# Later q/k load, shorter float64 conversion and earlier weight fetches in a fused attention and low-rank-mixing MLP kernel

## The chip, the cores and the metric

The kernel runs on one core of a Trainium2 chip. The time is device microseconds of one execution; 817.39 us is the median of three executions (816.22 to 820.38).

## What is computed

Attention with a relative-position bias runs over 4 batches, 8 heads, 576 positions and 64 channels a head; its result, with heads side by side, goes through a low-rank mixing over positions and a two-layer MLP, each with a residual.

```python
scores = scale * q @ k.T                                # per batch and head
x = log1p(|i - j|) / log1p(max(i, 1))
scores += (maximum(x * w1 + b1, 0.0) @ w2)[head]        # 32 hidden units
attn = exp(scores - max); attn = attn / (attn.sum() + 1e-09)
x = concat_heads(attn @ v)                              # [4, 576, 512] float32
u = x + (x.T @ U @ V).T                                 # U, V are float64, rank 32
out = float32(u + maximum(u @ w_ch1, 0.0) @ w_ch2)      # weights are float64
```

The float64 arrays (U, V and both weights, 512 by 2048 and 2048 by 512) come to the chip as pairs of 32-bit words and are turned into float32 there.

## The kernel before, in words

The kernel has an order written out by hand. Each engine works through its own instructions in that order, and SyncE (SP) issues all DMAs in one queue, so that a DMA that waits holds up those behind it.

The bias stage comes first. 36 steps (the loop over `order`) each make four `ring` tiles of hidden units (one on ScalarE, three on VectorE, `bias_hid`), multiply them with `w2` on TensorE (`bias_mm`), scale on ScalarE and store to `bias_dram` (`bias_out`). `bias_loads` fetches the bias again, in the order that attention wants, when the rows are there. Slots 0 to 3 of head pair 0 are woven into this loop (`early`).

Attention then works through 16 pairs of heads (four a batch), nine slots each. `load_pair` brings q and k of a pair into the tile `raw`, of which there is one buffer. `prep_ops` splits it into a rounded part (`hi`) and a remainder (`lo`) in four steps, on GpSimd for all pairs but pair 0, into tiles with two buffers. `scores` multiplies, adds the bias and takes the extreme on VectorE; `exps` takes the exponential and its sum on ScalarE; `recip` adds 1e-9 to the sums and inverts them (slots 0, 4 and 8) and scales the 64 left-over rows of the pair into `pm` on GpSimd. Transposes (`tr`, `tr_m`, `tr_mid`), the product with v (`av`) and `assemble` follow in later slots. After every slot `background(1)` emits one group from `queue`.

`queue` holds the float64 conversions, 256 columns each. `conv_ops` makes one: a load into `wraw` (three buffers), `size`, `clamp`, `shift`, `join` and `power` on VectorE, `low` on ScalarE, `scale` and `add` on GpSimd. `pipeline` makes five groups of each. 20 of them run beside attention (U, V and the first quarter of the weights, which goes to `wq_dram`), 48 beside the MLP stage, with two groups a step.

Pairs 5, 9, 13 also carry the mixing of the batch before (`mix_t`, `mix_h`, whose result goes to `u_dram`). From pair 13 on `first_weights` fetches the converted first quarter again from `wq_dram`, and `split` makes its two parts on ScalarE and GpSimd. The MLP stage (`mlp1`, `mlp2`) goes over nine blocks of 256 rows for each of four quarters.

Of the kernel before, what the change touches and what calls it, by code (L numbers as in the profile page):

```python
# [8 lines left out]
F32 = mybir.dt.float32  # L9
F32R = mybir.dt.float32r  # L10
I32 = mybir.dt.int32
# [31 lines left out]
def kernel(  # L43
# [34 lines left out]
    const = ctx.enter_context(tc.tile_pool(name="const", bufs=1, side="left"))  # L78
    qkp = ctx.enter_context(tc.tile_pool(name="qkp", bufs=2, side="left"))
    wcp = ctx.enter_context(tc.tile_pool(name="wcp", bufs=2, side="left"))  # L80
    wrawp = ctx.enter_context(tc.tile_pool(name="wrawp", bufs=3, side="left"))
    p1 = ExitStack()
    mix = p1.enter_context(tc.tile_pool(name="mix", bufs=1, side="left"))
# [8 lines left out]

    ident = const.tile([P, P], F32, name="ident")
    sgn = const.tile([P, 1], I32, name="sgn")
    u_sb = mix.tile([P, 5, RANK], F32, name="u_sb")
    v4h = mix.tile([P, 640], F32R, name="v4h")
    v4l = mix.tile([P, 640], F32R, name="v4l")
# [55 lines left out]

    def conv_ops(src, n, finish):
        st = {}

        def load():
            st["raw"] = wrawp.tile([P, CW], I64, tag="wraw", name="wraw")  # L160
            nc.sync.dma_start(out=st["raw"][:, 0:n], in_=src)
            words = st["raw"].bitcast(I32).rearrange("p (n t) -> p n t", t=2)
            st["l"], st["h"] = words[:, 0:n, 0], words[:, 0:n, 1]

        def size():
            st["t"] = wcp.tile([P, CW], I32, tag="t", name="wt")[:, 0:n]
            nc.vector.tensor_scalar(
                out=st["t"], in0=st["h"], scalar1=0x7FFFFFFF, scalar2=None, op0=ALU.bitwise_and
            )

        def clamp():
            nc.vector.tensor_scalar(
                out=st["t"].bitcast(F32), in0=st["t"].bitcast(F32),
                scalar1=F64_LO, scalar2=F64_HI, op0=ALU.max, op1=ALU.min,
            )

        def shift():
            nc.vector.tensor_scalar(
                out=st["t"], in0=st["t"], scalar1=3, scalar2=0x3FFFFFF8,
                op0=ALU.logical_shift_left, op1=ALU.bitwise_and,  # L180
            )

        def join():
            nc.vector.scalar_tensor_tensor(  # L184
                out=st["t"], in0=st["h"], scalar=sgn, in1=st["t"], op0=ALU.bitwise_and, op1=ALU.bitwise_or
            )

        def low():
            st["y"] = wcp.tile([P, CW], F32, tag="wy", name="wy")[:, 0:n]
            nc.scalar.activation(out=st["y"], in_=st["l"].bitcast(U32), func=AF.Copy, scale=2.0**-52)  # L190

        def power():
            st["e"] = wcp.tile([P, CW], I32, tag="e", name="we")[:, 0:n]
            nc.vector.tensor_scalar(  # L194
                out=st["e"], in0=st["t"], scalar1=-8388608, scalar2=None, op0=ALU.bitwise_and
            )

        def scale():
            nc.gpsimd.tensor_tensor(out=st["y"], in0=st["y"], in1=st["e"].bitcast(F32), op=ALU.mult)  # L199

        def add():
            nc.gpsimd.tensor_tensor(out=st["y"], in0=st["y"], in1=st["t"].bitcast(F32), op=ALU.add)

        return load, [size, clamp, shift, join, low, power, scale, add], lambda: finish(st["y"])


    tabp = p1.enter_context(tc.tile_pool(name="tabp", bufs=1, side="left"))
# [78 lines left out]
    def scores(p, s):  # L286
# [35 lines left out]
        )  # L322
        d["dst"] = dst

    def exps(p, s):
        d = pair[p]
        st, dst = d["st"], d["dst"]
        nc.scalar.activation(  # L328
            out=dst, in_=dst, func=AF.Exp, bias=st[:, s : s + 1], scale=-1.0, accum_out=st[:, 10 + s : 11 + s]
        )  # L330

    def recip(p, s):
        d = pair[p]
        st = d["st"]
        if s in (0, 4, 8):
            n = 1 if s == 0 else 4
            rec = st[:, 20 + s - n + 1 : 21 + s]
            nc.vector.tensor_scalar(  # L338
                out=rec, in0=st[:, 10 + s - n + 1 : 11 + s], scalar1=1.0e-9, scalar2=None, op0=ALU.add
            )  # L340
            nc.vector.reciprocal(out=rec, in_=rec)
        if s == 0:
            pm = pmp.tile([P, S + LEFT], F32, tag="pm", name="pm")
            for o, i, n in ((0, 0, S), (S, S - LEFT, LEFT)):
                nc.gpsimd.tensor_scalar(
                    out=pm[:, o : o + n],
                    in0=d["praw"][:, i : i + n],
                    scalar1=st[:, 20:21],
                    scalar2=1.0,
                    op0=ALU.mult,  # L350
                    op1=ALU.mult,
                )
            d["pm"] = pm

    def copy(eng, out, in_):
# [254 lines left out]
    def pipeline(jobs):  # L610


        ops = [conv_ops(*j) for j in jobs]
        groups = [[ops[0][0], ops[1][0]]]
        end = None
        for i, (_, o, fin) in enumerate(ops):
            if i + 2 < len(ops):
                groups[-1].append(ops[i + 2][0])
            size, clamp, shift, join, low, power, scale, add = o
            groups += [[size], [clamp], [shift], [join, low], [power, scale, add]]  # L620
            if end is not None:
                groups[-3].append(end)
            end = fin
        return groups + [[], [end]]

# [22 lines left out]
    pools["pt"] = p1.enter_context(tc.tile_pool(name="ptp", bufs=1, side="left"))  # L648
    nc.sync.dma_start(out=ident, in_=ident_in)
    nc.vector.memset(sgn.bitcast(F32), -2.0)  # L650
    load_pair(0)
    load_v(0)
    new_pair(0)
# [4 lines left out]
    for i in range(len(order) + 2):  # L658
# [15 lines left out]
        del loads[:2]  # L674
        if 8 <= i < 12:
            prep.pop(0)()
        if i == 20:
            load_pair(1)
        if i in early:
            slot(0, early[i])  # L680
# [1 line left out]
    psT2 = ctx.enter_context(tc.tile_pool(name="psT2", bufs=2, space=PSUM))  # L682
    rot = {"s": [psS], "t": [psT, psT2, psT2]}
    loads[0:0] = bias_loads(3, 0)
    loads += [o for c in (4, 0, 1, 2, 3) for o in bias_loads(c, 1)]


    jobs = [(u32, 160, fin_u)]
    jobs += [(v4[:, a : min(a + CW, 640)], min(CW, 640 - a), fin_v(a, min(a + CW, 640))) for a in range(0, 640, CW)]
    jobs += weight_jobs(0, lambda g, which, k, a, e: fin_w(wq_dram[4 * which + k, :, a:e]))  # L690
    queue += pipeline(jobs)
    queue[1:1] = [[]] * 8

    def big_views(t, parts):
        views, o = [], 0
# [3 lines left out]
        return views  # L699

    def first_weights(which):
        for k in range(KD):
            y = wrawp.tile([P, CW], I64, tag="wraw", name="y0").bitcast(F32)
            nc.sync.dma_start(out=y, in_=wq_dram[4 * which + k])
            yield
            split(0, which, k, 0, DM)(y)

    feed = iter(())
    for p in range(NP):
# [3 lines left out]
            bias[p + 1] = big.tile([P, 9 * S], F32, tag=f"big{p + 1}", name=f"bias{p + 1}")  # L713
            loads = [o for c in (4, 0, 1, 2, 3) for o in bias_loads(c, p + 1)]
        for s in range(9):
            if s == (1 if p else 4) and p < NP - 1:
                prep = prep_ops(p + 1)
            if s in ((2, 3, 4, 5) if p else (4, 5, 6, 7)) and p < NP - 1:
                prep.pop(0)()
            if s == (7 if p else 8) and p < NP - 2:  # L720
                load_pair(p + 2)
            if s == 7 and p + 1 < NP:
                load_v(p + 1)
# [3 lines left out]
            if p > 0 or s not in early.values():  # L727
                if p > HP and p % HP == 1 and s == 0:
                    mix_t(p // HP - 1)
                slot(p, s)  # L730
                background(1)
            if p > HP and p % HP == 1:
                for c in {1: (4,), 2: (0,), 3: (1,), 4: (2,), 5: (3,)}.get(s, ()):
                    mix_h(p // HP - 1, c)
# [173 lines left out]
```

## Time and profile before

| | |
|---|---|
| median of three executions | 817.39 us |
| the profiled execution | 813.02 us |
| its span, first to last instruction | 811.2 us |
| mean granted share of TensorE's clock | 0.981 |
| TensorE busy | 762.2 us, 94% |
| VectorE busy | 522.3 us, 64% |
| ScalarE busy | 329.7 us, 41% |
| GpSimd busy | 288.0 us, 36% |

The table is of one execution, and its shares are means over stages that are unlike each other. A busy TensorE is not TensorE at its peak, since matmuls are pipelined and the time that one waits in the pipeline counts as busy. A matmul at the lower of the two clocks takes longer and counts as busy, too.

### The profile page before, as it was taken

What the parts mean: (1) busy time and instruction counts of PE and PEld (TensorE: products, weight loads), DVE (VectorE), ACT (ScalarE), POOL (GpSimd) and SP (SyncE); (2) the same over time, 40 slices, a digit from 0 to 9 for tenths busy, and PEclk for the clock granted to TensorE, in tenths of its full rate; (3) what the DMA queues carried; (4) which work ended last, traced back from release to release, by engine and by line L of the source; (5) the groups of instructions that cost most, each with busy time, mean ns of one, the idle gap of its engine ahead of it and who ended that gap; (6) DMA issues with size and microseconds to landing.
All of it is one profiled execution on the core that took longest, in us unless ns stands there. A gap on an engine that the chain in (4) does not pass through costs nothing.

```text
span 811.2 us, 13968 instructions
## 1 busy us (share of the span) xinstructions
PE 762.2 (94%) x5292; PEld 623.5 (77%) x5292; DVE 522.3 (64%) x1144; ACT 329.7 (41%) x701; POOL 288.0 (36%) x289
## 2 busy tenths in 40 slices
PE   6979597889889999979999999999999999999998
PEld 3427475657666777757878999999999999999996
DVE  8996388877997999646335987666616666212222
ACT  7967455655565666657312332222201222100110
POOL 0050455554665566553001655244503454000000
PEclk9989898999999999999999999999999999999999
DMA  7768885245445544644005211112101120001111
GB/s 222 243 225 273 248 249 133 67 127 144 117 107 147 144 104 91 176 130 160 2 20 195 79 63 55 40 53 64 54 1 40 53 65 14 1 27 53 53 40 65
DMA packets 39299, 84.02 MB, mean 104 GB/s; under 512 B 6720, under 2 KB 9408, under 8 KB 37184
## 3 DMA queue, kind: packets, MB, share of 16 engines
q1 hardware_dynamic: 39232, 83.13, 35.3%
q8 instruction: 42, 0.69, 0.4%
q14 instruction: 25, 0.20, 0.1%
HBM read 60.96 MB, written 22.15 MB: 102 GB/s over the span
## 4 chain that ended last, share of the span: by engine, by line
PE 72%; DVE 13%; DMA 7%; ACT 3%; issue 3%; POOL 1%; SPq 1%; DVEq 0%; ACTq 0%; POOLq 0%
PE ph L562 25%; PE po L585 24%; PE sc L311 6%; PE o L413 5%; PE tb L377 4%; DVE p L313 3%; DMA raw<-in_qk_dram 2%; DVE ring L238 2%; PE o L421 2%; DVE pt L359 1%; DVE wt L184 1%; DMA bias_dram<-ring 1%; DVE st L338 1%; PE bs L247 1%; ACT p L328 1%
## 5 line engine op out<-in xcount | busy, mean ns | idle before, releaser
L328 ACT ACTIVATE p<-p,st 128x576 f32<-128x576 f32 x128 | 99.8, 780 | 70.4 <-DVE st L313 67.4
L199 POOL TENSOR_TENSOR wy<-wy,we 128x256 f32<-128x256 f32 (+1 forms) x68 | 49.8, 732 | 211.8 <-DVE we L194 181.3
L311 PE MATMUL sc<-hi 128*128 128x288 f32 x320 | 106.4, 348 | 11.2 <-POOL hi L137 6.5
L313 DVE CUSTOM_DVE_ANT_0 p<-sc,bias 128x576 f32<-128x576 f32 x128 | 96.0, 750 | 32.3 <-PE sc L311 27.2
L568 DVE SCALAR_TENSOR_TENSOR hh<-ph,hh 128x1024 fp32r<-128x1024 f32 x36 | 44.1, 1225 | 112.9 <-ACT hh L567 112.7
L585 PE MATMUL po<-w2q,hh 128*128 128x512 f32 x432 | 102.2, 392 | 0.0
L585 PE MATMUL po<-wq,hh 128*128 128x512 f32 x432 | 101.1, 390 | 0.0
L567 ACT ACTIVATE hh<-ph 128x1024 fp32r<-128x1024 f32 x36 | 36.9, 1024 | 152.6 <-PE ph L562 152.6
L562 PEld LDWEIGHTS ph<-ut,wq 128*128 128x128 f32 x768 | 93.4, 190 | 1.3
L562 PE MATMUL ph<-ut,wq 128*128 128x256 f32 x768 | 93.7, 281 | 0.0
L311 PE MATMUL sc<-lo,hi 128*128 128x288 f32 x320 | 91.2, 301 | 2.6 <-POOL lo L143 2.6
L562 PE MATMUL ph<-ut,w1q 128*128 128x256 f32 x768 | 93.4, 280 | 0.0
L562 PEld LDWEIGHTS ph<-ut,w1q 128*128 128x128 f32 x768 | 91.3, 188 | 1.9 <-issue 0.8
L585 PEld LDWEIGHTS po<-w2q,hh 128*128 128x128 f32 x432 | 80.0, 188 | 16.4
L585 PEld LDWEIGHTS po<-wq,hh 128*128 128x128 f32 x432 | 80.0, 188 | 15.9
L588 DVE TENSOR_TENSOR acc<-po,acc 128x512 f32<-128x512 f32 x72 | 49.6, 690 | 61.6 <-PE po L585 61.3
L311 PEld LDWEIGHTS sc<-hi 128*128 128x128 f32 x320 | 62.1, 194 | 30.3 <-issue 9.2
L377 PE MATMUL tb<-ident,p 128*128 128x128 f32 x512 | 79.7, 279 | 5.5 <-ACT p L328 4.7
L413 PE MATMUL o<-pt,v 128*64 128x256 f32 (+1 forms) x512 | 76.7, 421 | 0.0
L377 PEld LDWEIGHTS tb<-ident,p 128*128 128x128 f32 x512 | 63.2, 144 | 7.8 <-ACT p L328 6.2
L311 PEld LDWEIGHTS sc<-lo,hi 128*128 128x128 f32 x320 | 62.2, 194 | 5.2 <-POOL lo L143 3.2
L357 ACT COPY pt<-tb 128x512 f32<-128x512 f32 x88 | 50.9, 579 | 37.4 <-PE tb L377 37.4
(94 smaller groups left out, 1160.7 us busy)
## 6 DMA issues: line engine op xcount, KB each, us to landing
raw<-in_qk_dram SPq DMA_DIRECT2D x32, 608.0 KB, 7.6
wraw<-in_w_ch_dram SPq DMA_DIRECT2D x64, 256.0 KB, 2.7
bias_dram<-ring SPq DMA_DIRECT2D x36, 288.0 KB, 3.1
v<-in_vp_dram SPq DMA_DIRECT2D x16, 320.0 KB, 7.9
bias<-bias_dram SPq DMA_DIRECT2D x16, 288.0 KB, 4.4
acc<-u_dram SPq DMA_DIRECT2D x18, 256.0 KB, 4.8
out_dram<-acc SPq DMA_DIRECT2D x18, 256.0 KB, 2.0
bias<-bias_dram SPq DMA_DIRECT2D x16, 256.0 KB, 4.3
```

Of the source, the lines that this page charges most:

```text
L199: nc.gpsimd.tensor_tensor(out=st["y"], in0=st["y"], in1=st["e"].bitcast(F32), op=ALU.mult)
L311: mm(ps[:, a, 0:HALF], lhsT=hi[:, q0 : q0 + P], rhs=kk, start=(i == 0), stop=(i == n - 1))
L313: nc.vector.tensor_tensor_reduce(out=halves(dst), in0=ps[:, :, 0:HALF], in1=halves(bias[hp][:, s * S : (s + 1) * S]), scale=-0.125, scalar ...
L328: nc.scalar.activation(out=dst, in_=dst, func=AF.Exp, bias=st[:, s : s + 1], scale=-1.0, accum_out=st[:, 10 + s : 11 + s])
L357: nc.scalar.copy(out=out, in_=in_)
L377: nc.tensor.transpose(bank[:, kb, :], src[:, b0 + kb * P : b0 + (kb + 1) * P], ident)
L413: mm(o[hd * D : (hd + 1) * D, 0:n], lhsT=v[:, (4 * hd + j) * D : (4 * hd + j + 1) * D], rhs=pt[:, 5 * hd + j, :], start=(j == 0), stop=False,)
L562: mm(st["ps"][:, f, :], lhsT=w, rhs=u[:, k, :], start=(i == 0), stop=(i == 3 * KD - 1))
L567: nc.scalar.activation(out=hh[n], in_=st["ps"], func=AF.Relu)
L568: nc.vector.scalar_tensor_tensor(out=hl[n], in0=st["ps"], scalar=0.0, in1=hh[n].bitcast(F32), op0=ALU.max, op1=ALU.subtract)
L585: mm(ps, lhsT=h, rhs=w, start=(m == 0), stop=(m == 3 * FG - 1))
L588: nc.vector.tensor_tensor(out=a, in0=ps, in1=a, op=ALU.add)
```

## The change

The load of pair 1's q and k moves from step 20 of the bias loop to step 31, and its split on GpSimd from slots 4 to 7 of pair 0 to slots 0 to 3. The load of pair 2 moves from slot 8 of pair 0 into the list of bias loads, ahead of the last three of pair 1.

A conversion loses `power` on VectorE and `scale` on GpSimd. `size` becomes an Abs on ScalarE, `low` gives a whole number (scaled by 2^-29) in one of four buffers of a new pool, and `add` adds whole numbers on GpSimd. A conversion has three groups instead of five. Beside attention, groups are emitted after slots 0, 1, 6, 7 (two) and 8 alone, and two empty groups instead of eight stand ahead.

The addition of 1e-9 moves from VectorE into `exps`, as an Identity with a bias on ScalarE. The `pm` scaling of pair 0 moves from GpSimd to ScalarE.

`first_weights` starts a fetch two steps ahead of its `split`, in six steps at slots 1, 2, 4, 5, 7 and 8 instead of five at even slots.

```diff
+    wyp = ctx.enter_context(tc.tile_pool(name="wyp", bufs=4, side="left"))
...
+    eps = const.tile([P, 1], F32, name="eps")
...
         def size():
             st["t"] = wcp.tile([P, CW], I32, tag="t", name="wt")[:, 0:n]
-            nc.vector.tensor_scalar(
-                out=st["t"], in0=st["h"], scalar1=0x7FFFFFFF, scalar2=None, op0=ALU.bitwise_and
-            )
+            st["y"] = wyp.tile([P, CW], I32, tag="wy", name="wy")[:, 0:n]
+            nc.scalar.activation(out=st["t"].bitcast(F32), in_=st["h"].bitcast(F32), func=AF.Abs)
+
+        def low():
+            nc.scalar.activation(out=st["y"], in_=st["l"].bitcast(U32), func=AF.Copy, scale=2.0**-29)
...
-        def low():
-            st["y"] = wcp.tile([P, CW], F32, tag="wy", name="wy")[:, 0:n]
-            nc.scalar.activation(out=st["y"], in_=st["l"].bitcast(U32), func=AF.Copy, scale=2.0**-52)
-
-        def power():
-            st["e"] = wcp.tile([P, CW], I32, tag="e", name="we")[:, 0:n]
-            nc.vector.tensor_scalar(
-                out=st["e"], in0=st["t"], scalar1=-8388608, scalar2=None, op0=ALU.bitwise_and
-            )
-
-        def scale():
-            nc.gpsimd.tensor_tensor(out=st["y"], in0=st["y"], in1=st["e"].bitcast(F32), op=ALU.mult)
-
         def add():
-            nc.gpsimd.tensor_tensor(out=st["y"], in0=st["y"], in1=st["t"].bitcast(F32), op=ALU.add)
+            nc.gpsimd.tensor_tensor(out=st["y"], in0=st["t"], in1=st["y"], op=ALU.add)
...
+    def sums(st, s):
+        n = 1 if s == 0 else 4
+        return st[:, 11 + s - n : 11 + s], st[:, 21 + s - n : 21 + s]
...
+        if s in (0, 4, 8):
+            total, rec = sums(st, s)
+            nc.scalar.activation(out=rec, in_=total, func=AF.Identity, bias=eps)
...
-            nc.vector.tensor_scalar(
-                out=rec, in0=st[:, 10 + s - n + 1 : 11 + s], scalar1=1.0e-9, scalar2=None, op0=ALU.add
-            )
+            rec = sums(st, s)[1]
             nc.vector.reciprocal(out=rec, in_=rec)
...
+                if p == 0:
+                    nc.scalar.activation(out=pm[:, o : o + n], in_=src, func=AF.Copy, scale=st[:, 20:21])
...
-            groups += [[size], [clamp], [shift], [join, low], [power, scale, add]]
+            groups += [[size, low, clamp], [shift], [join, add]]
             if end is not None:
-                groups[-3].append(end)
+                groups[-2].append(end)
...
-        if i == 20:
+        if i == 31:
             load_pair(1)
...
-    loads += [o for c in (4, 0, 1, 2, 3) for o in bias_loads(c, 1)]
+    loads += [o for c in (4, 0, 1, 2) for o in bias_loads(c, 1)] + [lambda: load_pair(2)] + bias_loads(3, 1)
...
-    queue[1:1] = [[]] * 8
+    queue[1:1] = [[]] * 2
+
+    conv_at = {0: 1, 1: 1, 6: 1, 7: 2, 8: 1}
...
     def first_weights(which):
-        for k in range(KD):
-            y = wrawp.tile([P, CW], I64, tag="wraw", name="y0").bitcast(F32)
-            nc.sync.dma_start(out=y, in_=wq_dram[4 * which + k])
+        ys = []
+        for k in range(KD + 2):
+            if k < KD:
+                ys.append(wrawp.tile([P, CW], I64, tag="wraw", name="y0").bitcast(F32))
+                nc.sync.dma_start(out=ys[k], in_=wq_dram[4 * which + k])
+            if k >= 2:
+                split(0, which, k - 2, 0, DM)(ys[k - 2])
             yield
-            split(0, which, k, 0, DM)(y)
...
-            if s == (1 if p else 4) and p < NP - 1:
+            if s == (1 if p else 0) and p < NP - 1:
                 prep = prep_ops(p + 1)
-            if s in ((2, 3, 4, 5) if p else (4, 5, 6, 7)) and p < NP - 1:
+            if s in ((2, 3, 4, 5) if p else (0, 1, 2, 3)) and p < NP - 1:
                 prep.pop(0)()
-            if s == (7 if p else 8) and p < NP - 2:
+            if s == 7 and 0 < p < NP - 2:
                 load_pair(p + 2)
...
-                background(1)
+                background(conv_at.get(s, 0))
...
-            if p >= NP - 3 and s % 2 == 0:
+            if p >= NP - 3 and s in (1, 2, 4, 5, 7, 8):
                 next(feed, None)
```

## Rows read from the trace of the kernel before

**Rows 1.** Stages: borders, length, busy time of each engine (instructions), granted clock, DMA.
```profile
0.00:74.40 74.40, 61.03 (x656) 31.48 (x656) 64.78 (x141) 58.59 (x95) 13.25 (x10) 0.95 0.73 230
74.40:100.30 25.90, 17.26 (x123) 13.39 (x123) 12.24 (x40) 14.23 (x35) 8.99 (x7) 0.88 0.96 287
100.30:163.90 63.60, 56.08 (x367) 42.75 (x369) 53.30 (x129) 35.63 (x87) 35.37 (x31) 0.91 0.58 149
163.90:248.70 84.80, 76.45 (x515) 56.98 (x515) 72.23 (x177) 49.21 (x118) 47.18 (x38) 0.98 0.49 125
248.70:324.20 75.50, 73.90 (x519) 55.92 (x521) 65.44 (x176) 49.33 (x120) 45.84 (x38) 1.00 0.47 118
324.20:388.20 64.00, 58.73 (x405) 45.28 (x406) 37.51 (x108) 39.93 (x95) 30.46 (x23) 0.97 0.51 148
388.20:811.20 423.00, 418.76 (x2721) 377.70 (x2719) 216.80 (x377) 82.78 (x155) 106.92 (x144) 1.00 0.15 50
```
**Rows 2.** Chain of waits, bias stage: start, length, what.
```profile
38.32 8.21 DMA bias_dram<-ring
...
54.95 3.00 DVE ring L238
...
67.81 2.50 DMA bias_dram<-ring
```
**Rows 3.** Timeline of SyncE's queue, to 101 us: start, length, instruction.
```profile
8.98 10.60 SPq L259 DMA_DIRECT2D bias_dram<-ring  x8
...
37.10 0.48 SPq L116 DMA_DIRECT2D raw<-in_qk_dram  x1
...
54.23 7.03 SPq L259 DMA_DIRECT2D bias_dram<-ring  x2
...
81.23 0.48 SPq L116 DMA_DIRECT2D raw<-in_qk_dram  x1
...
100.32 0.48 SPq L116 DMA_DIRECT2D raw<-in_qk_dram  x1
```
**Rows 4.** Timeline of GpSimd, to 109 us; in brackets idle time before and its releaser.
```profile
46.00 4.48 POOL L137 TENSOR_SCALAR hi<-raw 128x1216 fp32r<-128x1216 f32 x1 [6.16 <-DMA raw<-in_qk_dram]
...
54.80 2.83 POOL L143 TENSOR_TENSOR lo<-raw,hi 128x1216 fp32r<-128x1216 f32 x1
...
92.10 1.21 POOL L137 TENSOR_SCALAR hi<-raw 128x1216 fp32r<-128x1216 f32 x1 [12.26 <-DMA raw<-in_qk_dram]
...
97.55 2.75 POOL L143 TENSOR_TENSOR lo<-raw,hi 128x1216 fp32r<-128x1216 f32 x1
...
108.97 1.21 POOL L137 TENSOR_SCALAR hi<-raw 128x1216 fp32r<-128x1216 f32 x1 [1.91 <-DMA raw<-in_qk_dram]
```
**Rows 5.** Timeline of TensorE around the start of pair 2.
```profile
97.52 0.61 PE L311 MATMUL sc<-hi 128*128 128x288 f32 x1 [6.47 <-POOL hi L137]
100.35 0.61 PE L311 MATMUL sc<-lo,hi 128*128 128x288 f32 x1 [2.22 <-POOL lo L143]
```
**Rows 6.** VectorE's groups, 164 to 249 us: busy us, mean ns | idle before.
```profile
L338 DVE TENSOR_SCALAR st<-st 128x4 f32<-128x4 f32 x8 | 5.7, 715 | 0.0
L167 DVE TENSOR_SCALAR wt<-wraw 128x256 int32<-128x256 int32 x7 | 5.5, 791 | 0.0
...
L194 DVE TENSOR_SCALAR we<-wt 128x256 int32<-128x256 int32 x7 | 4.7, 676 | 0.0
```
**Rows 7.** Chain of waits, pair 14.
```profile
346.20 8.83 DMA y<-wq_dram
```
**Rows 8.** Timeline of VectorE: first scores of pairs 11 and 12.
```profile
291.13 0.75 DVE L313 CUSTOM_DVE_ANT_0 praw<-sc,bias 128x576 f32<-128x576 f32 x1
...
308.30 0.74 DVE L313 CUSTOM_DVE_ANT_0 praw<-sc,bias 128x576 f32<-128x576 f32 x1
```
**Rows 9.** ScalarE's groups over the span, as in rows 6.
```profile
L190 ACT ACTIVATE wy<-wraw 128x256 f32<-128x256 uint32 x66 | 28.6, 434 | 7.0 <-DMA wraw<-in_w_ch_dram 7.0
...
L213 ACT ACT_TABLE_LOAD x1 | 1.3, 1283 | 0.7 <-PEq L897 0.7
```

More of the change, by code (lines that the diff above doesn't have):

```diff
@@ L186, in join @@
             )
-        def low():
-            st["y"] = wcp.tile([P, CW], F32, tag="wy", name="wy")[:, 0:n]
-            nc.scalar.activation(out=st["y"], in_=st["l"].bitcast(U32), func=AF.Copy, scale=2.0**-52)
-        def power():
-            st["e"] = wcp.tile([P, CW], I32, tag="e", name="we")[:, 0:n]
-            nc.vector.tensor_scalar(
-                out=st["e"], in0=st["t"], scalar1=-8388608, scalar2=None, op0=ALU.bitwise_and
-            )
-        def scale():
-            nc.gpsimd.tensor_tensor(out=st["y"], in0=st["y"], in1=st["e"].bitcast(F32), op=ALU.mult)
         def add():
-            nc.gpsimd.tensor_tensor(out=st["y"], in0=st["y"], in1=st["t"].bitcast(F32), op=ALU.add)
-        return load, [size, clamp, shift, join, low, power, scale, add], lambda: finish(st["y"])
+            nc.gpsimd.tensor_tensor(out=st["y"], in0=st["t"], in1=st["y"], op=ALU.add)
+        return load, [size, low, clamp, shift, join, add], lambda: finish(st["y"].bitcast(F32))
     tabp = p1.enter_context(tc.tile_pool(name="tabp", bufs=1, side="left"))
@@ L335, in recip @@
         if s in (0, 4, 8):
-            n = 1 if s == 0 else 4
-            rec = st[:, 20 + s - n + 1 : 21 + s]
-            nc.vector.tensor_scalar(
-                out=rec, in0=st[:, 10 + s - n + 1 : 11 + s], scalar1=1.0e-9, scalar2=None, op0=ALU.add
-            )
+            rec = sums(st, s)[1]
             nc.vector.reciprocal(out=rec, in_=rec)
@@ L344, in recip @@
             for o, i, n in ((0, 0, S), (S, S - LEFT, LEFT)):
[L345 to L352, printed above, removed]
+                src = d["praw"][:, i : i + n]
+                if p == 0:
+                    nc.scalar.activation(out=pm[:, o : o + n], in_=src, func=AF.Copy, scale=st[:, 20:21])
+                else:
+                    nc.gpsimd.tensor_scalar(
+                        out=pm[:, o : o + n], in0=src, scalar1=st[:, 20:21], scalar2=1.0, op0=ALU.mult, op1=ALU.mult
+                    )
             d["pm"] = pm
@@ L618, in pipeline @@
                 groups[-1].append(ops[i + 2][0])
-            size, clamp, shift, join, low, power, scale, add = o
-            groups += [[size], [clamp], [shift], [join, low], [power, scale, add]]
+            size, low, clamp, shift, join, add = o
+            groups += [[size, low, clamp], [shift], [join, add]]
             if end is not None:
-                groups[-3].append(end)
+                groups[-2].append(end)
             end = fin
@@ L650 @@
     nc.vector.memset(sgn.bitcast(F32), -2.0)
+    nc.vector.memset(eps, 1.0e-9)
     load_pair(0)
```

## The prediction

> **What bounds the kernel now.** I read the stages first [rows 1]. The borders are points where TensorE begins something: the first scores of pair 1 (74.4) and of pair 2 (100.3), the mixing steps of batches 0, 1 and 2 (163.9, 248.7, 324.2), the first MLP matmul (388.2). From 388.2 on TensorE is busy 418.76 of 423.00 us at full clock, so nothing that this change does to ScalarE, VectorE or GpSimd there can win more than a few us. What can be won lies in the first 388 us. There the seven rows are not alike: in 74.4 to 100.3 TensorE works 17.26 of 25.90 us; in 100.3 to 163.9 it has idle time and a granted clock of 0.91, a mean of stretches at 2.4 and at 1.2 GHz; in 163.9 to 248.7 VectorE is busy 72.23 of 84.80; 248.7 to 324.2 holds the same four pairs' worth of work (one batch, one mixing step) and takes 75.50. The same work at 84.8 and at 75.5 says that 163.9 to 248.7 is not bound by TensorE's work but by what it waits for.
>
> Next the chain of waits and the timelines, for who is late. Three things stand out.
>
> First, the loads of q/k. The tile `raw` has one buffer, so load p+1 waits until GpSimd has split pair p. Pair 1's load goes out at 37.10 [rows 3], and a bias store behind it needs 8.21 us to land where the last one needs 2.50 [rows 2]. GpSimd then splits pair 1 in the middle of the bias stage; while its 2.83 us subtraction runs from 54.80 [rows 4], one VectorE `ring` step takes 3.00 us, from 54.95 [rows 2], and the 30th bias store, at 54.23, is followed by the next only some 6.7 us later (the two fill the 7.03 us of their row), against 10.60 us for the first eight, 1.3 each [rows 3]; stores 31 to 36 come after it. Pair 2's load goes out only at 81.23 [rows 3], its split runs from 92.10 to 100.30 [rows 4], and TensorE waits 6.47 + 2.22 us for it [rows 5].
>
> Second, VectorE steps that read SBUF at speed stand still while GpSimd works. In 163.9 to 248.7 the tiny add of 1e-9 takes 715 ns on average and a 256-wide conversion step 676 to 791 ns [rows 6]; the chain runs through them, because scores, exponentials and transposes of the next slots wait behind them on VectorE.
>
> Third, the `y` load of the first weights: at 346.20 the chain waits 8.83 us for it [rows 7], which had been queued behind pair 15's q/k and v.
>
> **The change part by part.** The profiled execution took 813.0 us (span 811.2 and 1.8 around it); the median shown is 817.4. I sum differences and take them from the median.
>
> *q/k load of pair 1 at step 31 instead of 20; pair 2's as 19th instead of 21st transfer after the last bias store.* Step 31 comes after the 30th store, 54.23 [rows 3]; the `pm` scaling of pair 0, now on ScalarE, puts about 1 us more (640 columns at `low`'s 0.43 us for 256 [rows 9]) into a stretch where ScalarE and VectorE are both full, so about 55. Landing: 37.10 to 46.00 is 8.9 us [rows 3, 4], with the same stores around it, so 64. The split without collision takes 8.2 (92.10 to 100.30), so 72.2. Without the collision the six stores that are left come at 1.3 us, the last near 62 instead of 67.8 [rows 2]; but now the q/k load lies among them and the store may need 8.21 instead of 2.50 to land, so 65 to 70, take 67. Three bias loads (some 3 us, an estimate from the 2.50 of a store of their size) end at 70 to 71, pair 0's last slots near 72. Both paths let pair 1 start at 72 to 73 instead of 74.4. Pair 2's load: 18/20 of the 10.9 us from 70.3 (2.50 after 67.81) to 81.23, so 67 + 9.8 = 77; it lands 10.9 later (81.23 to 92.10), 88; split 8.2; pair 2 starts at 96 instead of 100.3. Term: −5. Ends: −9 (the store lands in 2.50) and +2 (the tail of the bias stage crowded by the load).
>
> *Conversion.* Of five VectorE steps `size` (now Abs on ScalarE) and `power` go, of two GpSimd steps `scale` goes, and the adds of 1e-9 go to ScalarE. In 163.9 to 248.7 that is 5.5 + 4.7 + 5.7 = 15.9 us of VectorE in four pairs [rows 6], 4 us a pair; what is left, one step a slot, is emitted in slots 0, 1, 6, 7, 8, away from slots 2 to 5, where GpSimd's split is emitted. Added: per conversion one ScalarE step like `low`, 0.43 us [rows 9]; per pair three tiny additions, each under that 0.43; ScalarE is at 49.21 of 84.80 [rows 1] and goes from 12.3 to at most 14.5 us a pair. A new wait: `clamp` on VectorE now waits for ScalarE's Abs, which stands behind that slot's exponential and copies, and the next slot's scores wait behind `clamp`. No row shows it. Low end 0 (ScalarE ahead), high end an Abs and another such step ahead of it, 2 × 0.43, twice a pair, 1.7 us; I take 0.5 a pair, because ScalarE idles more than a third of this stage; it lies within the lengths below. The integer add on GpSimd isn't in the trace either; the float adds it replaces fit in GpSimd's idle 37 us of that stage, and at double their price still would.
>
> Pairs 5 to 8 then have what pairs 9 to 12 have. I take TensorE's busy time of that later group, 73.9 [rows 1], as their length: 84.8 − 73.9 gives −10.9; ends −5 (collisions stay in part) and −13.5 (four pairs near pair 11's 17.17 [rows 8], and a mixing step). Pairs 9 to 12: 75.5 to 73.9, −1.6; ends 0 and −3.5. Pairs 2 to 4 take 63.6 now. Their bound is the loop of one `raw` buffer: load 100.32 to 108.97, 8.65 us [rows 3, 4], and split 8.2, so 16.9 us a pair when no conversion stands between; but the split then lies in the second half of the pair, where conversions are emitted too. I take 18 each: 54.0, −9.6; ends −4.5 (19.7 each) and −12.6 (17.0 each).
>
> The Trainium skill (SBUF — State Buffer, "Who interferes with whom") says that VectorE and GpSimd share one pair of ports, held as an exclusive lock, and that a VectorE step with two SBUF inputs or in a two-port mode takes part in it. The 3.00 us step above, ending as the 2.83 us subtraction does, agrees. By that rule all three remaining conversion steps stay exposed, which speaks for the first rival below.
>
> *First weights two steps ahead.* The transfer has two slots to land and goes out before pair 15's q/k. 324.2 to 388.2 has 58.73 busy of 64.0: −5.5; ends −4 and −8.
>
> *MLP stage.* Conversions go through in three groups a job instead of five, at two groups a step, so they come denser; TensorE covers them (418.76 of 423.00). 0; ends +2 and −1.
>
> Sum: −5 − 9.6 − 10.9 − 1.6 − 5.5 = −32.6, so 817.4 − 32.6 = 784.8.
>
> **The rivals.** (a) The collisions move rather than go: with `raw` as a loop, GpSimd's split drifts into slots 6 to 8, onto the conversion steps. For it: pairs 2 to 4 are at the loop's pace. Against it: 12 exposed steps a pair (nine of conversions, three additions) become 6. Then the low ends of pairs 2 to 8 hold: −5 − 4.5 − 5 + 0 − 5.5 = −20, so 797.
>
> (b) TensorE is as bound as its busy share says, and only the two long waits go: half of the 8.7 us before pair 2 and the `y` wait, −4.5 − 5.5 = −10, so 807. For it: TensorE's busy time in 163.9 to 248.7 is 76.45 of 84.80. Against it: 75.5 for the same work later; a busy row there includes matmuls waiting in the pipeline.
>
> (c) Slower: Abs and the tiny additions need another function table than the exponential's. The trace shows one load, 1.283 us [rows 9]. Two loads, to and back, at two conversions and three additions a pair are 5 × 2.57 = 12.8 us; ScalarE would go from 12.3 to 26.6 us a pair, over the present 21.2, and 15 pairs would lose about 80 us: 897. It decides from 8.9 us of loads a pair on, some seven loads. Against it: one load serves Relu, Exp and Copy now. The Trainium skill (ScalarE: Activation LUTs, "Table sets: the hidden batching unit") says that relu, copy, identity and abs are in every set; by that rule no load is added. No run here shows Abs.
>
> (d) The loads stay as late as they are and only VectorE's relief counts: −32.6 + 5 + 4 = −23.6, so 794.
>
> **How the numbers follow.** Chances: forecast 0.60, (a) 0.18, (d) 0.09, (b) 0.08, (c) 0.02, a better case than the forecast, all low ends together (−9 − 12.6 − 13.5 − 3.5 − 8 = −46.6, 771), 0.03. The range reaches from 768 to 802: it holds the forecast with its ends, (a) and (d), and leaves out (b) and (c). By cases 0.98 end faster; I keep 0.03 of it for what the trace doesn't show. 0.5%, about 4 us, is what a measurement of this kernel can tell from no change: faster 0.95, same 0.02, slower 0.03.
>
> **What would show it.** Right: pair 1's split on GpSimd after the last `ring` step; no `ring` step of 2 to 3 us; pair 2's first scores near 96; four pairs with a mixing step in 74 us; no wait of ScalarE for `y`; one table load; the MLP stage still 423 us. Wrong: the last bias store landing at 70 or later; conversion steps of over 2 us in slots 6 to 8; VectorE idle before `clamp`, waiting for ScalarE; pairs 6 to 8 at 19 us or more.

## The result, and the profile after

The changed kernel took 792.84 us, the median of four executions (792.01 to 794.81), against 817.06 for the kernel before on the same chip: a ratio of 0.970, 95% interval 0.967 to 0.973. The forecast was 784.8 (768 to 802). So the sign and the range were right, and 8 of the 32.6 us forecast did not come. The profiled execution took 792.01 us, its span is 790.2 (before 811.2). Of the ten executions of e7 below two were slow ones (816.26 and 816.71 us, over 1.5% above its fastest), and its time and ratio leave them out.

The stages of the kernel after, from the view that gives each stretch its length, busy time of each engine (and instructions), granted clock, DMA share and GB/s. The borders are the events of [rows 1], its first two rows taken together: pair 2's first scores, the mixing steps of batches 0, 1 and 2, the first MLP matmul.

```profile
0.00:100.00 100.00, 77.99 (x778) 45.39 (x778) 70.70 (x173) 75.05 (x137) 17.69 (x16) 0.95 0.80 243
100.00:156.20 56.20, 52.49 (x367) 39.35 (x367) 39.48 (x117) 40.61 (x105) 31.65 (x25) 1.00 0.67 177
156.20:231.20 75.00, 73.67 (x515) 55.99 (x513) 52.73 (x151) 54.58 (x139) 42.29 (x32) 1.00 0.54 141
231.20:305.10 73.90, 73.08 (x519) 55.93 (x520) 50.41 (x145) 53.66 (x136) 39.98 (x29) 1.00 0.47 118
305.10:362.30 57.20, 56.68 (x404) 43.73 (x403) 35.73 (x99) 42.28 (x104) 29.29 (x22) 1.00 0.58 165
362.30:790.20 427.90, 423.65 (x2723) 380.60 (x2721) 173.61 (x280) 99.08 (x204) 71.12 (x96) 1.00 0.15 49
```

| stage | before | after | measured | forecast (ends) |
|---|---|---|---|---|
| to the first scores of pair 2 | 100.3 | 100.0 | −0.3 | −5 (−9 to +2) |
| pairs 2 to 4 | 63.6 | 56.2 | −7.4 | −9.6 (−12.6 to −4.5) |
| pairs 5 to 8 | 84.8 | 75.0 | −9.8 | −10.9 (−13.5 to −5) |
| pairs 9 to 12 | 75.5 | 73.9 | −1.6 | −1.6 (−3.5 to 0) |
| pairs 13 to 15 | 64.0 | 57.2 | −6.8 | −5.5 (−8 to −4) |
| MLP | 423.0 | 427.9 | +4.9 | 0 (−1 to +2) |
| sum | 811.2 | 790.2 | −21.0 | −32.6 |

The spans differ by 21.0, the medians by 24.2: the profiled execution of the kernel before (813.02) lay 4 us under its median. Two rows do not fit: the front brought nothing, and the MLP stage, where nothing was to change, became 4.9 us longer with TensorE busy for all of it (423.65 of 427.90, against 418.76 of 423.00 in [rows 1]). TensorE does the same matmuls there; many of them take longer.

First the front: the chain of waits (start, length, what), SyncE's queue and GpSimd (idle time before it and its releaser in brackets), answering [rows 2 to 4].

```profile
56.65 7.69 DMA bias_dram<-ring
...
64.40 6.04 DMA bias_dram<-ring
...
82.43 11.19 DMA bias<-bias_dram
```
```profile
55.00 0.48 SPq L118 DMA_DIRECT2D raw<-in_qk_dram  x1
...
70.52 6.84 SPq L267 DMA_DIRECT2D bias<-bias_dram  x14
...
80.30 0.48 SPq L118 DMA_DIRECT2D raw<-in_qk_dram  x1
```
```profile
63.98 1.21 POOL L139 TENSOR_SCALAR hi<-raw 128x1216 fp32r<-128x1216 f32 x1 [63.54 <-DMA raw<-in_qk_dram]
...
91.73 1.21 POOL L139 TENSOR_SCALAR hi<-raw 128x1216 fp32r<-128x1216 f32 x1 [4.82 <-DMA raw<-in_qk_dram]
...
97.20 2.79 POOL L145 TENSOR_TENSOR lo<-raw,hi 128x1216 fp32r<-128x1216 f32 x1
```

Pair 1's q/k goes out at 55.00 and lands at 63.98, where the forecast had 55 and 64, and GpSimd splits it behind the last `ring` step. The last store leaves 3.4 us earlier than before (64.40, before 67.81), and lands at 70.44, before at 70.31 [rows 2]: it needs 6.04 us instead of 2.50. The q/k transfer has landed by then, but it has delayed the stores behind it: in the chain the last store follows the landing of the one that left at 56.65, right behind q/k, and that one needed 7.69 us. The chain then runs through bias loads, the longest from 82.43 to 93.62. Pair 2's load leaves at 80.30 (before 81.23), its split begins at 91.73 (before 92.10).

In the same stretch a new wait shows on VectorE (first fence) and on ScalarE (second): the first conversion's Abs waits for its load, and `clamp` and pair 1's first scores wait behind it.

```profile
82.85 0.24 DVE L177 TENSOR_SCALAR wt<-wt 128x160 f32<-128x160 f32 x1 [7.25 <-ACT wt L171]
83.00 0.75 DVE L305 CUSTOM_DVE_ANT_0 praw<-sc,bias 128x576 f32<-128x576 f32 x1
```
```profile
82.47 0.35 ACT L171 ACTIVATE wt<-wraw 128x160 f32<-128x160 f32 x1 [5.63 <-DMA wraw<-in_u_dram]
```

ScalarE's groups over the span (busy us, mean ns of one, idle before): Abs takes 435 ns, an addition of 1e-9 takes 302 ns, and there is one table load as in [rows 9].

```profile
L171 ACT ACTIVATE wt<-wraw 128x256 f32<-128x256 f32 x66 | 28.7, 435 | 7.9 <-DMA wraw<-in_w_ch_dram 7.9
...
L329 ACT ACTIVATE st<-st,eps 128x4 f32<-128x4 f32 x32 | 9.7, 302 | 1.0
...
L205 ACT ACT_TABLE_LOAD x1 | 1.3, 1283 | 0.7 <-PEq L897 0.7
```

### The profile page after: what moved, and what is told of

It is laid out like the page before. It is cut to its first block, busy times and chain, and to the rows that moved or that the text cites. A ratio compares the mean times of both kernels' runs of the same rounds, so it can differ in the third digit from the quotient of the medians.

```text
span 790.2 us, 13762 instructions
## 1 busy us (share of the span) xinstructions
PE 757.6 (96%) x5292; PEld 621.0 (79%) x5292; DVE 422.7 (53%) x961; ACT 365.3 (46%) x819; POOL 232.0 (29%) x219
## 4 chain that ended last, share of the span: by engine, by line
PE 78%; ACT 7%; DVE 6%; DMA 5%; issue 3%; SPq 1%; DVEq 0%; ACTq 0%
PE ph L556 26%; PE po L579 25%; PE sc L303 7%; PE o L407 7%; PE tb L371 4%; DMA bias<-bias_dram 3%; ACT p L324 2%; PE o L415 2%; DMA bias_dram<-ring 2%; DVE p L305 1%; ACT ring L228 1%; DVE ring L230 1%; PE mt L448 1%; PE bs L239 1%; PE tu L529 1%
## 5 line engine op out<-in xcount | busy, mean ns | idle before, releaser
L324 ACT ACTIVATE p<-p,st 128x576 f32<-128x576 f32 x128 | 99.9, 781 | 43.4 <-DVE st L305 42.9
L194 POOL TENSOR_TENSOR wy<-wt,wy 128x256 int32<-128x256 int32 (+1 forms) x68 | 50.2, 738 | 214.3 <-DVE wt L189 187.5
L579 PE MATMUL po<-w2q,hh 128*128 128x512 f32 x432 | 104.0, 395 | 0.0
L556 PE MATMUL ph<-ut,w1q 128*128 128x256 f32 x768 | 95.7, 283 | 0.0
L556 PEld LDWEIGHTS ph<-ut,w1q 128*128 128x128 f32 x768 | 93.5, 189 | 2.0 <-issue 0.8
L579 PEld LDWEIGHTS po<-w2q,hh 128*128 128x128 f32 x432 | 79.9, 188 | 18.2
L371 PE MATMUL tb<-ident,p 128*128 128x128 f32 x512 | 77.8, 275 | 0.9 <-DVE pt L353 0.5
```

The lines of the kernel that those rows point to most:

```text
L194: nc.gpsimd.tensor_tensor(out=st["y"], in0=st["t"], in1=st["y"], op=ALU.add)
L324: nc.scalar.activation(out=dst, in_=dst, func=AF.Exp, bias=st[:, s : s + 1], scale=-1.0, accum_out=st[:, 10 + s : 11 + s])
L371: nc.tensor.transpose(bank[:, kb, :], src[:, b0 + kb * P : b0 + (kb + 1) * P], ident)
L556: mm(st["ps"][:, f, :], lhsT=w, rhs=u[:, k, :], start=(i == 0), stop=(i == 3 * KD - 1))
L579: mm(ps, lhsT=h, rhs=w, start=(m == 0), stop=(m == 3 * FG - 1))
```

## The experiments

Ratios are to the kernel before on the same chip, with the 95% interval; the stages are those of the table above.

**Why is the MLP stage longer?** The change brings one new tile of 4 bytes a row, `eps`, next to `sgn`. Every tile allocated behind it on that side of SBUF lies 32 bytes further: `hh`, `ut` of the last five blocks and one half of the fourth's, and the second and fourth quarter's weights (`wq`). The first and third quarter's weights (`w1q`, `w2q`) and the rest of `ut` lie on the other side and do not move. The first run takes that shift out of the kernel after, the second puts it alone into the kernel before, with a tile that nothing reads.

```diff
-    sgn = const.tile([P, 1], I32, name="sgn")
-    eps = const.tile([P, 1], F32, name="eps")
+    two = const.tile([P, 2], I32, name="sgn")
+    sgn, eps = two[:, 0:1], two[:, 1:2].bitcast(F32)
```

> The changed kernel, with the constant 1e-9 in a second column of the tile sgn instead of a tile of its own. In the changed kernel that tile of 4 bytes a partition moves every tile of the left side after it by 32 bytes; here all lie again where they lay before the change, and nothing else differs. Theory 'places': the 4.9 us that the MLP stage lost come from where the tiles lie; MLP stage from 427.9 back to 423 us, the whole about 788. Rival 'denser conversions': three groups instead of five, at two groups a step, slow the matmuls; then the MLP stage stays at 428 and the whole at 793.

Measured: 787.53 us, 0.965 (0.961 to 0.969); the MLP stage took 423.4.

```diff
+    pad = const.tile([P, 1], F32, name="pad")
...
+    nc.vector.memset(pad, 0.0)
```

> The kernel before, with one more constant tile of 4 bytes a partition behind sgn, filled once and never read: the same 32 bytes shift, no other change. Theory 'places': MLP stage from 423.0 to about 428 us, the whole from 817 to about 822. Rival 'denser conversions': 817, MLP stage 423.

Measured: 820.83 us, 1.005 (1.002 to 1.009); the MLP stage took 428.0. The MLP stage of both, e1 first (columns as in the stages above):

```profile
362.30:785.70 423.40, 419.16 (x2722) 377.95 (x2720) 173.80 (x280) 98.94 (x204) 71.03 (x96) 1.00 0.15 50
```
```profile
389.80:817.80 428.00, 423.70 (x2723) 380.64 (x2721) 216.97 (x377) 82.88 (x155) 107.01 (x144) 1.00 0.15 49
```

The clock is 1.00 in both. The chain shows where: a block of 48 first-layer matmuls (`ph`) and of 24 second-layer ones (`po`), late in the first quarter and, last row, late in the second. The kernel after, then e1 (in the first quarter its seventh block, then its sixth; both take `ut` from the side that moved):

```profile
443.37 5.69 PE ph L556 x48
449.05 5.59 PE po L579 x24
...
533.76 5.75 PE ph L556 x48
```
```profile
430.51 5.46 PE ph L556 x48
435.97 5.50 PE po L579 x24
...
531.64 5.75 PE ph L556 x48
```

A first-layer matmul takes 5.46/48 = 113.8 ns in e1 and 5.69/48 = 118.5 in the kernel after; a second-layer one 5.50/24 = 229 against 5.59/24 = 233. In the last blocks of the second quarter both need 5.75/48 = 119.8: there weights and `ut` lie on the same side and move together. So the pace of a matmul here depends on where its two inputs lie to each other, and one 4-byte tile costs the stage 4.5 to 5 us. Both runs say so, one in each direction. Why the place matters no run here shows.

**Why did the front bring nothing?** Two suspects: the conversion's new wait (7.25 us of VectorE, above), or the transfers. e3 gives the conversion's load the eight empty groups again that stood ahead before; e4 puts pair 1's load back to step 20.

```diff
-    queue[1:1] = [[]] * 2
+    queue[1:1] = [[]] * 8
```

> The changed kernel with eight empty groups instead of two ahead of the first conversion. The first Abs then no longer waits for its words, and VectorE's clamp no longer holds up pair 1's first scores (7.25 us at 75.6 to 82.9). Theory 'transfers': pair 1 starts some 7 us earlier, but pair 2 still waits for its split, which ends near 100 because its q/k land near 91.7; the second matmul of pair 2 stays at 99 to 101, and the whole within 1 us of 793. Rival 'the new wait is what the front lost': pair 2 starts 5 to 7 us earlier and the whole is 786 to 788.

Measured: 792.39 us, 0.971 (0.967 to 0.976), the time of the kernel after. The wait is gone (pair 1's first scores at 76.3 instead of 83.0), and pair 2 still starts when its split ends. Its second matmul in e3:

```profile
99.49 0.61 PE L303 MATMUL sc<-lo,hi 128*128 128x288 f32 x1 [2.22 <-POOL lo L145]
```

The wait of 7.25 us costs nothing as long as pair 2's q/k comes this late.

```diff
-        if i == 31:
+        if i == 20:
             load_pair(1)
```

> The changed kernel with pair 1's q/k loaded at step 20 again, the rest as changed. GpSimd's split falls back into the bias stage (ring steps of 2 to 3 us). Theory 'transfers': from 55 us on the transfers are the bound, and it is the same bytes that must be moved before pair 2's q/k, so pair 2's split ends at 99 to 102 as well; the whole 792 to 795. Rival, the first term of the prediction: the later load is worth about 5 us through the collisions that it avoids, so the whole is 797 to 799.

Measured: 792.55 us, 0.972 (0.967 to 0.977). The collision is back and so is the old order of the stores (chain):

```profile
51.74 3.00 DVE ring L230
...
67.03 3.61 DMA bias_dram<-ring
```
A `ring` step takes 3.00 us again, the last store leaves at 67.03 instead of 64.40, and lands at 70.64 against 70.44. Pair 2's split ends at 99.9, in the kernel after at 100.0. The move of pair 1's load, then, takes away a real stall and is worth nothing here: what it frees on VectorE is given back in the transfers. The stretch in which pair 2's load goes out and lands, in the kernel after:

```profile
74.40:101.30 26.90, 20.27 (x133) 15.43 (x134) 13.14 (x38) 15.52 (x39) 10.36 (x9) 0.87 1.00 281
```

A DMA share of 1.00 at 281 GB/s: pair 2's load is one more transfer where no room is left.

**What are the parts of the attention's gain?** First the parts alone, on the kernel before. e5 has only `first_weights` with its six slots:

```diff
-        for k in range(KD):
...
+        for k in range(KD + 2):
...
+            if k >= 2:
+                split(0, which, k - 2, 0, DM)(ys[k - 2])
             yield
-            split(0, which, k, 0, DM)(y)
...
-            if p >= NP - 3 and s % 2 == 0:
+            if p >= NP - 3 and s in (1, 2, 4, 5, 7, 8):
```

> The kernel before with the fetches of the first weights two steps ahead and nothing else. Theory: this alone gives what 324.2 to 388.2 lost in the changed kernel, 6.8 us; that stage goes from 63.9 to about 57, the whole from 817 to about 810.5. Rival: pairs 13 to 15 were shortened by the adds on ScalarE as well, so that this alone gives only the wait for y, 4 to 5 us, and the whole is 812 to 813.

Measured: 809.28 us, 0.993 (0.990 to 0.996). Pairs 13 to 15 of e5:

```profile
324.80:384.50 59.70, 57.14 (x405) 43.84 (x404) 38.40 (x108) 39.70 (x95) 32.57 (x24) 1.00 0.54 161
```

64.0 to 59.7 is −4.3 in the stage, the rival's 4 to 5 and not the theory's 6.8; the kernel after comes to 57.2. The early fetch carries about two thirds of this stage's −6.8. The next run, with the additions alone, has 60.9 us there, −3.1, so these are the likely rest; the two were not tried together.

e6 has only the additions of 1e-9 on ScalarE, with `eps` where it moves no other tile:

```diff
...
+            total, rec = sums(st, s)
+            nc.scalar.activation(out=rec, in_=total, func=AF.Identity, bias=eps)
...
-            nc.vector.tensor_scalar(
-                out=rec, in0=st[:, 10 + s - n + 1 : 11 + s], scalar1=1.0e-9, scalar2=None, op0=ALU.add
-            )
+            rec = sums(st, s)[1]
```

> The kernel before with the adds of 1e-9 on ScalarE (the constant in a second column of sgn, so that no tile moves) and nothing else. Theory 'each exposed VectorE step costs what it stands still': 29 adds of four columns took 15.3 us in all where 0.17 each would be 5, so up to 10 us of the chain go; the whole 808 to 812, most of it between 100 and 249 us. Rival: the stall only passes to the next exposed step (recip stands between two conversion steps), so less than 4 us.

Measured: 813.49 us, 0.997 (0.995 to 1.000). From 101 us to the mixing of batch 2 the kernel before (first fence) has these rows on VectorE, and e6 (second) those:

```profile
L172 DVE TENSOR_SCALAR wt<-wt 128x256 f32<-128x256 f32 x18 | 9.8, 542 | 0.1
...
L338 DVE TENSOR_SCALAR st<-st 128x4 f32<-128x4 f32 x22 | 13.1, 596 | 0.0
```
```profile
L173 DVE TENSOR_SCALAR wt<-wt 128x256 f32<-128x256 f32 x18 | 20.2, 1124 | 0.1
```

13.1 us of additions are gone from VectorE, and `clamp` alone rises from 9.8 to 20.2, the five conversion steps together by 10.8. Most of the 596 ns of a 128x4 addition was not its own price: the stall passes to another conversion step. It does not pass to every step that reads SBUF: the reciprocal of the same 128x4 sums takes 169 ns in e6 and 180 before. The small total hides larger differences: pairs 5 to 8 take 82.1 us (84.8 before), pairs 9 to 12 80.7 (75.5) and pairs 13 to 15 60.9 (64.0). Fewer steps of that kind do not help as long as others stand where GpSimd works.

The other way is to leave the steps and move them. e7 is e1 with its conversion groups in the middle slots; e9 is the kernel before, with its longer conversion, and its groups at the edges of the pair.

```diff
-    conv_at = {0: 1, 1: 1, 6: 1, 7: 2, 8: 1}
+    conv_at = {1: 1, 2: 1, 3: 1, 4: 1, 5: 1, 6: 1}
```

> The changed kernel with all tiles at the old places, and its six conversion groups a pair after slots 1 to 6 instead of 0, 1, 6, 7, 7, 8: as many steps, but now beside GpSimd's split. Theory 'placement': four to five VectorE steps a pair meet the split and stand still 1 to 2.7 us each, so that pairs 2 to 10 lose 1 to 2 us each; the whole 796 to 803 against 787.5. Rival 'number': what won was that there are fewer steps, not where they stand; the whole within 3 us of 787.5.

Measured: 805.96 us, the median of eight (803.65 to 815.37), 0.990 (0.986 to 0.995): 18.4 us more than e1, and more than the expected 796 to 803. Pairs 5 to 8 take 83.3 us (e1 75.9), pairs 9 to 12 79.9 (73.3), the stages behind them what they take in e1. VectorE's conversion steps from 101 to 305 us, the kernel after (the short conversion at the edges), then e7:

```profile
L189 DVE SCALAR_TENSOR_TENSOR wt<-wraw,sgn,wt 128x256 int32<-128x256 int32 x17 | 8.2, 483 | 0.3
...
L177 DVE TENSOR_SCALAR wt<-wt 128x256 f32<-128x256 f32 x17 | 6.8, 399 | 20.9 <-ACT wt L171 20.9
...
L183 DVE TENSOR_SCALAR wt<-wt 128x256 int32<-128x256 int32 x17 | 4.6, 272 | 0.0
```
```profile
L189 DVE SCALAR_TENSOR_TENSOR wt<-wraw,sgn,wt 128x256 int32<-128x256 int32 x17 | 17.2, 1011 | 0.3
...
L177 DVE TENSOR_SCALAR wt<-wt 128x256 f32<-128x256 f32 x17 | 16.3, 959 | 19.6 <-ACT wt L171 19.6
...
L183 DVE TENSOR_SCALAR wt<-wt 128x256 int32<-128x256 int32 x17 | 9.3, 547 | 0.0
```

The same number of conversions, and each step takes about twice as long in the slots where GpSimd splits. A group takes its load and store along when it moves; the wait before `clamp`, 20.9 and 19.6 us, says that late loads are not the difference.

```diff
+    conv_at = {0: 2, 1: 2, 6: 2, 7: 2, 8: 2}
...
-                background(1)
+                background(conv_at.get(s, 0))
```

> The kernel before with its conversion of five groups as it was, and only its groups placed otherwise: two after each of slots 0, 1, 6, 7, 8 and none after slots 2 to 5. Theory 'placement': most of what pairs 2 to 12 won comes from there; 84.9 us (pairs 5 to 8) go to 77 to 79, pairs 2 to 4 win 4 to 6, the whole 800 to 806. Rival 'number of steps': VectorE has as many steps as before, now doubled up, so the whole stays at 812 to 817.

Measured: 804.32 us, 0.987 (0.983 to 0.991): −11.1 us for the place alone. Pairs 5 to 8 of e9, and two of VectorE's rows:

```profile
158.90:237.90 79.00, 75.43 (x513) 55.93 (x513) 66.80 (x181) 49.02 (x120) 48.35 (x40) 1.00 0.51 136
```
```profile
L178 DVE TENSOR_SCALAR wt<-wt 128x256 int32<-128x256 int32 x18 | 5.0, 278 | 0.3
...
L172 DVE TENSOR_SCALAR wt<-wt 128x256 f32<-128x256 f32 x17 | 21.9, 1291 | 0.6
```

Pairs 5 to 8 take 79.0, between 84.8 and the 75.0 of the kernel after; the mixing of batch 0 comes 5.0 us earlier (158.9), and pairs 9 to 12 take 76.1, no less than the 75.5 before. The other conversion steps take 278 to 481 ns, but `clamp` takes 1291: one step carries most of the stall that is left. The work of GpSimd beside it is the last subtraction of the split, and the two end within 0.2 us of each other (VectorE, then GpSimd, in e9):

```profile
196.45 2.60 DVE L172 TENSOR_SCALAR wt<-wt 128x256 f32<-128x256 f32 x1
```
```profile
196.12 2.79 POOL L143 TENSOR_TENSOR lo<-raw,hi 128x1216 fp32r<-128x1216 f32 x1
```

The product of e9 and e5 is 0.980, e1 has 0.965: a ratio of 0.984, some 13 us, is left for the shorter conversion and the smaller parts together. These were not parted further.

**Can the front's time be had?** If transfers bind it, pair 2's q/k must go out ahead of other bytes. e8 is e1, with the eight empty groups of e3 and `load_pair(2)` ahead of the bias loads that pair 1 needs later.

```diff
-    loads += [o for c in (4, 0, 1, 2) for o in bias_loads(c, 1)] + [lambda: load_pair(2)] + bias_loads(3, 1)
+    loads += [o for c in (4, 0) for o in bias_loads(c, 1)] + [lambda: load_pair(2)]
+    loads += [o for c in (1, 2, 3) for o in bias_loads(c, 1)]
```

> The changed kernel with all tiles at the old places, eight empty groups ahead of the first conversion, and pair 2's q/k loaded ahead of the bias of pair 1's slots 3 to 8 instead of its last two. Theory 'transfers': the q/k then land near 81 instead of 91.7, the split ends near 89, and pair 2 starts at 92 to 95, bound by pair 1's own slots and its later bias; the whole 780 to 783. Rival: the bias that is now later holds up pair 1 by as much; pair 2 starts at 98 to 100 and the whole is 786 to 788.

Measured: 785.57 us, 0.963 (0.960 to 0.967), in neither of the two ranges, and beside e1's 0.965 no clear gain; the profiled span is 783.6, e1's 785.7. SyncE's queue and GpSimd in e8:

```profile
73.77 0.48 SPq L118 DMA_DIRECT2D raw<-in_qk_dram  x1
...
84.94 11.22 SPq L267 DMA_DIRECT2D bias<-bias_dram  x18
96.48 0.48 SPq L118 DMA_DIRECT2D raw<-in_qk_dram  x1
```
```profile
83.80 1.21 POOL L139 TENSOR_SCALAR hi<-raw 128x1216 fp32r<-128x1216 f32 x1 [3.96 <-DMA raw<-in_qk_dram]
```

The split begins at 83.80 instead of 91.73, and the `praw` step of pair 2 comes at 95.6 instead of 103.3 in e1. Then most of it is given back: pair 1 now waits for its bias (5.02 and 2.28 us), and pair 3's q/k, behind 18 bias loads, goes out at 96.48 only, so that pair 2 takes 22 us; the mixing of batch 0 comes at 152.8 instead of 155.9.

e10 spreads those bias loads, so that pair 3's load stands ahead of some of them:

```diff
-            if s == 7 and 0 < p < NP - 2:
+            if s == (6 if p == 1 else 7) and 0 < p < NP - 2:
...
-            for o in loads[0:2]:
+            take = 2 if p != 1 else 1 if s < 6 else 3
+            for o in loads[0:take]:
...
```

> The kernel of the run in which pair 2's q/k come earlier, and in it pair 3's q/k one slot earlier with half as many bias loads ahead of it, so that it goes out when GpSimd has split pair 2 (92.1) instead of at 96.5. Theory 'transfers': pair 3's split ends some 4 us earlier, pair 2 takes 18 to 19 us instead of 22.1, and the 3 us that were given back stay won; the whole 781 to 784 against 785.6. Rival: pair 2's bias is now late instead; 785 to 788.

Measured: 785.18 us, 0.963 (0.960 to 0.967), the time of e8 within its scatter, and the rival's 785 to 788. The load goes out 3 us earlier:

```profile
93.50 0.48 SPq L118 DMA_DIRECT2D raw<-in_qk_dram  x1
```

Pair 2 takes 18.5 us, as expected, but begins at 97.5 and not at 95.6, with pair 1 still waiting for its own bias (6.01 and 1.50 us); the mixing of batch 0 comes at 152.0, 0.8 us earlier. The profiled span is 782.0 (e8 783.6). The medians do not tell the two apart.

**Can the matmuls' pace be had?** The last blocks of the second and fourth quarters pay 119.8 ns even in e1. e11 (e8 with 832 bytes a row that nothing reads ahead of these weights) and e12 (e10 with 384, the number 96 in place of 208) move the weights against all `ut`:

```diff
+    pool("padp", 1).tile([P, 208], F32, name="pad")
     w3p = pool("w3p", 1)
```

> The kernel of the run in which pair 2's q/k come earlier, with 832 bytes left free ahead of the weight tiles of the odd quarters, so that they stand to the moving tiles ut as the even quarters' tiles do (192 bytes apart modulo 1024; now 0 apart). Theory 'places, relative': the first layer's matmuls of the odd quarters go from 119.8 to about 114 ns for blocks 4 to 8 and the others to what the even quarters show, so the MLP stage goes from 423.3 to 418 to 420 us and the whole from 785.6 to 781 to 783. Rival: only the place itself counts, not that of one to the other; 423 us and 785.

> The kernel with pair 3's q/k earlier and 384 bytes left free ahead of the weight tiles of the odd quarters, so that they are 0 apart modulo 1024 from none of the moving tiles. Theory 'places, relative', and that 0 apart modulo 1024 is the bad case: all blocks of the odd quarters' first layer near 113.5 ns, the MLP stage from 423.3 to 419 to 420 us, the whole from 785.2 to 781 to 782. Rival: other distances are bad as well (in the changed kernel 224 apart gave 118); some blocks at 117 to 120, the whole 783 to 786.

Measured: e11 785.01 us, 0.963 (0.960 to 0.967), MLP stage 422.5, where 418 to 420 was expected; e12 785.87 us, 0.963 (0.959 to 0.967), MLP stage 425.3. The second quarter's blocks in the chain, e11 and then e12, an early and a late one each:

```profile
486.02 5.75 PE ph L556 x48
...
519.67 5.46 PE ph L556 x48
```
```profile
484.19 5.45 PE ph L556 x48
489.64 5.58 PE po L579 x24
...
517.54 5.76 PE ph L556 x48
```

In e1 the first two blocks of that quarter take 5.44, the last five 5.75. In e11 it is the other way round: what the last five gain (5.75 to 5.46) the first ones, whose `ut` lies on the other side, lose. In e12 the first layer is nearly as in e1, and the second layer's blocks rise from 5.47 to 5.58. The place decides, and one pad for all weights only shifts who pays. Which bits of the addresses count these runs don't settle: the rule of e12, that only a distance of 0 modulo 1024 is bad, failed, since with 384 bytes of pad the late blocks still take 5.76.

e1, e8, e10, e11 and e12, between 785.0 and 787.5 us, are faster than both kernels; among them these runs tell no difference.

## Why the prediction was right, and where it was not

- **The front (−5 forecast, −0.3 measured) is a step that failed.** Its early terms held: load out near 55, landed at 64, no `ring` step of 3 us. What failed is "so 65 to 70, take 67" for the last store. It left at 64.40, not near 62, and landed at 70.44, which the text itself named as a sign of being wrong. From there pair 2's load followed as the text had it, 9.9 us behind (80.30; the forecast took 9.8), and landed 11.4 us later. Pair 1's first scores came at 74.47, as before, not at 72 to 73. The deeper fault is that the front was costed by its collisions, in which VectorE loses time, while the transfers set its end. The row of [rows 1] with a DMA share of 0.96 and 287 GB/s had that before the change. e4 shows it: collision back, time the same. This is rival (d), loads as late as they were; its 794 came nearest to the 792.84, though in part by chance, as (d) had no loss in the MLP stage and no weaker pairs 2 to 8, and its 4 us beside the front's 5 have no working. The sums of the term itself are loose: 96 instead of 100.3 is −4.3, not −5, and a store that lands in 2.50 would make it about −7, not −9.
- **Pairs 2 to 4 (−9.6, −7.4) and 5 to 8 (−10.9, −9.8) went the right way for the right reason, a little over-sized.** Pairs 2 to 4 took 18.7 us each, not 18, and pair 8 19.7, a length that the text had named as a sign of being wrong (pairs 6 and 7 took 17.2 and 17.6). The granted clock rose in pairs 2 to 4 from 0.91 [rows 1] to 1.00, which the forecast had no term for. e9 shows that the place of the conversion steps alone brings 5.0 us up to the mixing of batch 0 and 5.8 in pairs 5 to 8, more than half of the gain; e7 that without it the short conversion loses most of its worth; e6 that fewer exposed steps alone bring little. How the rest divides is open. The forecast summed VectorE's busy time that goes (15.9 us in four pairs) only as a support, and took the length from pairs 9 to 12; that choice was the good one. Had it taken the busy rows as the price, the additions alone (13.1 us here) would have been far too large: e6's ratio, 0.997, is some 2 us, and its interval includes no gain at all.
- **Pairs 9 to 12 (−1.6, −1.6) right.** TensorE is busy 73.08 of 73.90 us there. The stage is not safe from the steps all the same: e6 and e7 have 80.7 and 79.9 there.
- **Early weights (−5.5, −6.8): the right cause, and a number that is right in part by luck.** Alone they bring 4.3 us in the stage (e5), where the text's own 64.0 − 58.73 gives 5.3. The additions on ScalarE, which the sum counted for nothing here, bring 3.1 alone (e6).
- **The new wait of `clamp` (0.5 us a pair taken, 1.7 at most) was larger; what it cost is measured only for the first conversion.** In 101 to 305 us VectorE stands 20.9 us before 17 conversions, 1.2 us each, more than the high end's 0.86; the first one stood 7.25 us. e3 takes that one away and gains nothing. The other waits lie inside stages that come out within 0.9 us of TensorE's busy time from pair 9 on, so little of them is left to be had.
- **The MLP stage (0, +4.9) is the second step that failed.** "TensorE covers them" holds: the conversions cost nothing there (e1, 423.4). What was not looked at is that `eps` moves tiles. No view of the trace before shows what a tile's place is worth; its chain does show that equal matmuls run at different paces, since blocks of 48 take 5.46 and 5.75 us:

```profile
479.88 5.46 PE ph L562 x48
...
545.92 5.75 PE ph L562 x48
```

- **Rival (a)**, collisions into slots 6 to 8, did not happen in the kernel after: `join`, `clamp` and `shift` take 483, 399 and 272 ns there, and none of over 1.5 us is among them. **Rival (b)** fell with pairs 5 to 8. **Rival (c)** fell: one table load, with Abs and Identity in use. Its 26.6 us a pair do not follow from its terms (12.3 + 12.8 is 25.1), which changes nothing.

Taken together: −32.6, with 4.7 more at the front, 4.9 in the MLP stage, 2.2 and 1.1 in pairs 2 to 8 and 1.3 less in pairs 13 to 15, gives −21.0, the spans' difference.

## What to carry to other kernels

Before a stall is priced, ask what the stretch ends on: where the DMA share was 1.00 here, a freed engine step was worth nothing until a transfer left earlier, and then the transfers that it passed were late next. Where two engines disturb each other, move the steps out of each other's time before making fewer of them, because here the stall passed to another exposed step. And a new tile, however small, moves those behind it: keep their places, or compare the time of equal blocks of matmuls before and after.

## What was not expected of the hardware

- Equal matmuls at a granted clock of 1.00 run at several paces by the places of their two inputs in SBUF: 113.8, 118.5 and 119.8 ns among others in the first layer, 229 and 233 in the second. The pace changed in blocks whose two inputs moved against each other, and stayed where both moved together (last blocks of the second quarter); the cause is open. A shift of 32 bytes made 423 us into 428 (e1, e2).
- A stall beside GpSimd doesn't belong to one instruction: with 13.1 us of additions taken off VectorE, `clamp` took 10.4 us more (e6). But not every kind of step takes part: reciprocals of 128x4 stayed at 169 to 180 ns.
- A 128x4 addition on ScalarE takes 302 ns, a 128x256 Abs 435 ns: a sixty-fourth of the elements at two thirds of the time.
